# Moving two batches' transform stages by half a tile to a tile in a kernel that mixes a Fourier filter with routed experts

## Chip, core and metric

One core of one Trainium2 chip. The metric is the device time of one execution in microseconds, median of three runs. The program is built once; it computes everything in float32.

## What is computed

The reference filters a sequence in the frequency domain and sends each token through one of eight experts, chosen by a hash of its id:

```python
batch, seq, dim = (8, 2496, 256)
X = np.fft.rfft(x, axis=1)
F = (filt_r + 1j * filt_i)[None, :, :]
y = np.fft.irfft(X * F, n=x.shape[1], axis=1)
...
N, D, E, F = (19968, 256, 8, 1024)              # N = 8 * 2496 tokens
expert_idx = token_ids * np.int64(2654435761) % np.int64(E)
for e in range(E):
    mask = expert_idx == e
    h = np.maximum(y.reshape(N, D)[mask] @ w1[e], 0.0)
    out[mask] = h @ w2[e]
```

## The kernel before

The Fourier transform of 2496 = 39 x 64 points is done as matrix products with tables, in three stages per batch:

- stage 1 (`pa`): products of x with `wf`, evicted to a buffer in SBUF, which is then stored to a DRAM scratch `d1`;
- stage 2 (`pb`, filter, `pc`): `load2` brings `d1` back transposed (in the profile `mid<-d`), `forward` multiplies by `d_t` and VectorE applies the filter, `back` multiplies by `e_t`; the result is stored to a second scratch `d2`;
- stage 3 (`pd`): `load4` brings `d2` back transposed (`t<-d`), products with `wi_t`, and each row of tokens is scattered to its expert's place in the DRAM array `xs`.

```python
def stage1(self, u):
    ...
    self.products(wf_t, (NR, NR), 2 * NS, self.x[v][:, sl, :], self.t1[:, sl, :], nc.scalar.copy, u, "pa")
    if half == 1:
        eng = nc.scalar if self.b == 2 else nc.gpsimd
        moves = self.parts(self.d1, self.t1, v)
        if self.b == 2 and v > 0:
            put_off.extend(moves)            # batch 2: these stores are issued later, by ScalarE
            return
        for dram, chip in moves:
            eng.dma_start(out=dram, in_=chip)

def load2(self, g):
    t2 = slot("t2")
    for p in range(2):
        a0 = p * NS + SG * g
        nc.sync.dma_start(out=t2[p:P:2, :, :], in_=self.d1[:, a0:a0 + SG, :])
    self.t2[g] = t2

def load4(self, v):
    self.t4[v] = t4pool.tile([NK, XL, C], F32, name=f"t4_{self.b}_{v}", tag="t4")
    for dram, chip in self.parts(self.d2, self.t4[v], v):
        nc.sync.dma_start(out=chip, in_=dram)
```

Batches are numbered from 0: "the third batch" is batch 2, "the fourth" batch 3. The first two batches are transformed ahead of the main loop, on chip alone. The main loop then goes through tiles of 128 routed tokens, 159 of them without a condition. Each tile is an up product (`ups`, 32 matmuls), a down product (`dps`, 16) and a scatter of its rows to the output. The other six batches are transformed between the products of the tiles. The tiles come in four routing stages, and those of a routing stage need the tokens of two more batches: 30 tiles can run with batches 0 and 1, the next ones need batches 2 and 3 as well.

```python
def step(i):
    ht = work.tile([P, FP, TB], F32, name=f"ht_{i}", tag="ht")
    if i + 4 < NT:
        load(i + 4)                          # xg<-xs: the tokens of a tile (of a pair of tiles), on the sync queue
    numbers(i)
    while main and main[0][0] < i + .5:      # pieces of the transforms, by their times
        main.pop(0)[1]()
    up(i, ht)
    weights(i + 2, 0)                        # wts<-in_moe_w: loaded only if the expert changes
    if i + 1 < NSURE:
        turn(i + 1)                          # xt<-xg, VectorE
    while main and main[0][0] < i + 1:
        main.pop(0)[1]()
    down(i, ht)
    weights(i + 2, 1)
```

What is put between the products of which tile is set by hand: each piece has a time in units of tiles. A piece with time 8.55 is issued in tile 8 between up and down, one with 8.0 in tile 8 ahead of up. Negative times lie ahead of the loop. All loads are issued by the sync engine in the order of these times, and a load that must wait holds those behind it.

```python
def spaced(t0, t1, n):
    return [t0 + (t1 - t0) * u / n for u in range(n)]

def part1(b, at, loads=None):                # stage 1: times of its pieces, and of the loads of x
    bt = batches[b]
    if loads is None:
        loads = [at[2 * v] - 2.5 * (at[1] - at[0]) for v in range(NV)]
    return ([(at[u], lambda u=u: bt.stage1(u)) for u in range(NU)] +
            [(loads[v], lambda v=v: bt.load1(v)) for v in range(NV) if b > 0])

def part2(b, at, ready):                     # stage 2, and its loads: none ahead of "ready"
    bt = batches[b]
    if isinstance(ready, list):
        return ([(at[u], lambda u=u: bt.stage2(u)) for u in range(NS // 2 + 1)] +
                [(t, lambda g=g: bt.load2(g)) for g, t in enumerate(ready)])
    return ([(at[u], lambda u=u: bt.stage2(u)) for u in range(NS // 2 + 1)] +
            [(max(at[2 * g] - 4.5 * (at[1] - at[0]), ready), lambda g=g: bt.load2(g)) for g in range(NS // SG)])

def part3(b, at, ready=None):                # stage 3, and its loads: none ahead of "ready"
    ...
    return ([(at[u], lambda u=u: bt.stage3(u)) for u in range(NU)] +
            [(max(at[2 * v] - 2.5 * (at[1] - at[0]), ready), lambda v=v: bt.load4(v)) for v in range(NV)])
...
todo += [(-75.5, lambda: [nc.scalar.dma_start(out=dram, in_=chip) for dram, chip in put_off])]
todo += [(-76, lambda: begin())]             # the loads of the first four tiles
...
todo += [..., (14.6, pads)]                  # seven scatters of blank rows by GpSimd
```

Here `NU` = 6, `N_2` = 11, `NV` = 3. A piece of stage 2 with number u does `forward(u)` and then `back(u - 1)`.

Of the kernel before, what the change touches and what calls it, by code (L numbers as in the profile page):

```python
# [36 lines left out]
NU = (HN + XG) // XG  # L37
# [82 lines left out]
def kernel(  # L120
# [324 lines left out]
    def load_tables(part):  # L445
        if part < 2:

            nc.gpsimd.tensor_copy(junk[:], first.x[2 * part][0:1, 0, 0:1])
        sl = S_PARTS[part]
        nc.sync.dma_start(out=d_t[:, sl, :], in_=d_dram.ap()[:, sl, :])  # L450
        for k in range(2):
            load_filter(k, sl)
# [207 lines left out]
    def spaced(t0, t1, n):  # L660
        return [t0 + (t1 - t0) * u / n for u in range(n)]

    def part1(b, at, loads=None):
# [7 lines that stand above are left out]
    def part2(b, at, ready):  # L671
# [8 lines that stand above are left out]
    def part3(b, at, ready=None):  # L680
        bt = batches[b]
        if b < 2:
            return [(at[u], lambda u=u: bt.stage3(u)) for u in range(NU)]
        return ([(at[u], lambda u=u: bt.stage3(u)) for u in range(NU)] +
                [(max(at[2 * v] - 2.5 * (at[1] - at[0]), ready), lambda v=v: bt.load4(v)) for v in range(NV)])
# [4 lines left out]
    N_2 = NS // 2 + 1  # L690
# [8 lines left out]
    todo = [(t, lambda k=k: load_tables(k)) for k, t in enumerate((-160, -159, -157, -156))]  # L699
# [17 lines left out]
    todo += [(t, lambda k=k: weights(k // 2, k % 2)) for k, t in enumerate((-99, -98.9, -98.8, -98.7))]  # L717
    todo += [(-76, lambda: begin())]

    todo += part1(3, spaced(1.5, 6.5, NU), [-74.6, -74.5, 2.5]) + part1(4, spaced(15, 20.5, NU))  # L720
    todo += part1(5, spaced(21, 27, NU)) + part1(6, spaced(35, 44.5, NU)) + part1(7, spaced(50, 60, NU))
    todo += part2(2, spaced(.55, 6, N_2), [-75, -74.9, -74.8, -74.7, 1.2]) + part2(3, spaced(9.2, 15.7, N_2), 6.6)
    todo += part2(4, spaced(22, 31, N_2), 20.5) + part2(5, spaced(31.2, 46, N_2), 28)
    todo += part2(6, spaced(48, 62, N_2), 47) + part2(7, spaced(63.2, 80, N_2), 61)
    todo += part3(2, spaced(8, 14.5, NU), 5.8) + part3(3, spaced(17, 25, NU), 15.6)
    todo += part3(4, spaced(33, 44, NU), 31.5) + part3(5, spaced(49, 63, NU), 46.5)
    todo += part3(6, spaced(67, 83, NU), 62) + part3(7, spaced(84, 101, NU), 81)
    todo.sort(key=lambda t: t[0])
# [164 lines left out]
```

## Time and profile before

| | before |
|---|---|
| median of 3 runs | 1509.66 us (1508.82 to 1509.69) |
| span of the profiled run | 1507.1 us |
| granted TensorE clock, mean | 0.986 |
| the tile loop begins | 145.36 us |
| DMA engines, mean | 226.06 MB, 150 GB/s |

The profile names engines PE (TensorE matmul), PEld (TensorE weight load), DVE (VectorE), ACT (ScalarE), POOL (GpSimd) and SP (sync); SPq, ACTq and POOLq are what these engines' queues issue. `L799` is a line of the kernel. "out<-in" names what an instruction writes and reads, and x32 is the number of instructions of a group. Times are microseconds from the start of the span. In a list of waits, a line says who waited for whom, then the total, how often and the longest. In a timeline a line is start, length, engine, line, operation, count, and in brackets how long the engine was idle before it and what ended that. One line of matrix product in the kernel appears as two matmul records for each product of float32, so four `pb` are the two products of one piece.

Two places in the kernel before which the change touches: the pieces of batch 2's stage 2 begin in tile 0 (the first has time 0.55), with their loads and then the loads of x for batch 3 ahead of the loop; and the pieces of batch 3's stage 3 begin at tile 17, with their first load in tile 15.

### The profile page before, as it was taken

The page shows a single profiled execution, that of the slowest core. Times are in us where ns is not written, and L with a number is a line of the kernel's source. Part 1 is how long each engine was busy: PE and PEld are TensorE (multiplying, and loading weights), DVE is VectorE, ACT ScalarE, POOL GpSimd, SP SyncE. Part 2 cuts the span into 40 slices and gives each one's busy share as a digit, 9 for nine tenths or more (in the row PEclk, how much of TensorE's full clock was granted, in tenths as well). Part 3 has the DMA queues.
Part 4 walks back from the last instruction along what each step waited for, and adds up shares of the span by engine and source line. Part 5 has one row for each costly group of instructions (what it writes and reads, how often), then busy time and mean ns, then how long its engine had stood idle before and what let it go on. Part 6 is the DMA issues. An engine that isn't in the chain of part 4 may idle for free.

```text
span 1507.1 us, 25818 instructions
## 1 busy us (share of the span) xinstructions
PE 1454.8 (97%) x9340; PEld 1338.0 (89%) x9340; DVE 538.4 (36%) x1008; ACT 234.6 (16%) x401; POOL 495.2 (33%) x802
## 2 busy tenths in 40 slices
PE   6996899989999999999999999999999999999997
PEld 6885789988899998899899999899999999999996
DVE  5972444622444444143434442222222222212221
ACT  3653120111121111011111110000000000000000
POOL 6465123544422344233422433234212111111211
PEclk9998999999999999999999999999999999999998
DMA  8266758668855954846647623653422423132321
GB/s 225 56 203 179 250 181 216 231 174 247 245 178 181 270 149 116 241 134 195 178 124 204 194 96 117 164 157 91 138 57 61 131 88 90 48 109 71 98 86 28
DMA packets 186988, 226.06 MB, mean 150 GB/s; under 512 B 101653, under 2 KB 157389, under 8 KB 180890
## 3 DMA queue, kind: packets, MB, share of 16 engines
q1 hardware_dynamic: 154615, 146.92, 35.1%
q0 software_dynamic: 28096, 73.51, 15.1%
q10 hardware_dynamic: 4147, 3.94, 0.9%
q8 instruction: 76, 1.25, 0.3%
q14 instruction: 54, 0.44, 0.1%
HBM read 415.94 MB, written 75.08 MB: 326 GB/s over the span
## 4 chain that ended last, share of the span: by engine, by line
PE 90%; DMA 5%; DVE 2%; issue 1%; POOL 1%; SPq 0%; ACT 0%; ACTq 0%; POOLq 0%; DVEq 0%
PE ups L799 36%; PE dps L811 35%; PE pd L228 5%; PE pb L273 4%; PE pc L295 3%; PE pa L228 3%; DMA wts<-in_x_dram 1%; PE pc L345 1%; DMA wts<-in_moe_w_dram 1%; DMA t<-d 1%; DMA d_t<-d_tbl 1%; DMA d<-mid 1%; DMA mid<-d 1%; PE pu L360 1%; DVE z L282 1%
## 5 line engine op out<-in xcount | busy, mean ns | idle before, releaser
L799 PEld LDWEIGHTS ups<-xt,wts 128*128 128x128 f32 x5088 | 596.4, 193 | 22.4 <-POOL no L782 10.6
L799 PE MATMUL ups<-xt,wts 128*128 128x128 f32 x5088 | 597.8, 276 | 11.6 <-DVE xt L789 10.1
L811 PE MATMUL dps<-wts,ht 128*128 128x256 f32 x2544 | 577.0, 380 | 0.1
L811 PEld LDWEIGHTS dps<-wts,ht 128*128 128x128 f32 x2544 | 475.8, 191 | 62.0 <-ACT mid L298 0.8
L815 POOL DMA_INDIRECT out_dram<-osb,no x159 | 158.2, 995 | 555.3 <-DVE osb L814 461.1
L805 DVE TENSOR_SCALAR ht<-ups 128x512 f32<-128x512 f32 x159 | 110.0, 692 | 484.6 <-PE ups L799 478.4
L803 ACT ACTIVATE ht<-ups 128x512 f32<-128x512 f32 x159 | 94.9, 597 | 867.4 <-PE ups L799 852.9
L391 POOL DMA_INDIRECT xs<-o,sidx x176 | 176.6, 1003 | 98.2 <-issue 44.3
L814 DVE COPY osb<-dps 128x256 f32<-128x256 f32 x159 | 67.5, 425 | 365.5 <-PE dps L811 364.1
L782 POOL COPY no<-xg 32x2 int32<-32x2 int32 (+1 forms) x328 | 59.9, 183 | 269.0 <-DMA out_dram<-osb,no 183.2
L282 DVE TENSOR_TENSOR z<-pb,filt 64x512 f32<-64x512 f32 x160 | 110.1, 688 | 2.3
L228 PE MATMUL pd<-t,wi_t 120*117 120x256 f32 x320 | 77.9, 387 | 5.4 <-DMA t<-d 4.1
L789 DVE STREAM_TRANSPOSE xt<-xg 128x256 f32<-128x256 f32 x159 | 69.0, 434 | 14.7 <-DMA d<-mid 14.7
L228 PEld LDWEIGHTS pd<-t,wi_t 120*117 120x117 f32 x320 | 57.4, 183 | 18.2 <-issue 5.5
L298 ACT COPY mid<-pc 128x512 f32<-128x512 f32 x60 | 35.2, 586 | 233.3 <-PE pc L295 232.2
L279 DVE TENSOR_TENSOR y<-pb,filt 128x512 f32<-128x512 f32 x80 | 54.2, 678 | 47.7 <-PE pb L273 47.2
L273 PE MATMUL pb<-mid,d_t 128*128 128x256 f32 x240 | 63.8, 389 | 7.0 <-DMA mid<-d 7.0
L283 DVE TENSOR_TENSOR y<-y,z 128x512 f32<-128x512 f32 x80 | 61.2, 766 | 2.7
L295 PE MATMUL pc<-y,e_t 128*128 128x256 f32 x240 | 61.7, 379 | 0.0
L273 PEld LDWEIGHTS pb<-mid,d_t 128*128 128x128 f32 x240 | 44.3, 195 | 13.0 <-issue 5.4
L228 PE MATMUL pa<-x,wf_t 117*120 117x256 f32 x224 | 52.7, 379 | 0.0
L295 PEld LDWEIGHTS pc<-y,e_t 128*128 128x128 f32 x240 | 45.4, 190 | 6.5 <-issue 0.4
(123 smaller groups left out, 548.9 us busy)
## 6 DMA issues: line engine op xcount, KB each, us to landing
wts<-in_moe_w_dram SPq DMA_DIRECT2D x320, 1024.0 KB
mid<-d SPq DMA_DIRECT2D x60, 256.0 KB
d<-mid POOLq DMA_DIRECT2D x60, 256.0 KB, 3.9
xg<-xs SPq DMA_DIRECT2D x235, 64.0 KB
t<-d SPq DMA_DIRECT2D x12, 960.0 KB
x<-in_x_dram SPq DMA_DIRECT2D x36, 312.0 KB
d<-mid POOLq DMA_DIRECT2D x10, 960.0 KB, 8.8
xg<-xs SPq DMA_DIRECT2D x77, 65.0 KB
```

The lines of the kernel that those rows point to most:

```text
L228: nc.tensor.matmul(out=ps[0:cols * H, k, :], lhsT=w[:], rhs=src[:, 2 * i + k, :], start=True, stop=True)
L273: nc.tensor.matmul(out=ps[:, i, :], lhsT=d_t[:, s, :], rhs=rhs, start=True, stop=True)
L282: nc.vector.tensor_tensor(out=z[b], in0=ps[a], in1=f_t[1][a, sl, :], op=OP.mult)
L295: nc.tensor.matmul(out=ps[:, i, :], lhsT=e_t[:, 2 * u + i, :], rhs=pr[:, i, :], start=True, stop=True)
L391: st = nc.gpsimd.indirect_dma_start(out=xs[:], out_offset=bass.IndirectOffsetOnAxis(ap=index, axis=0), in_=rows, in_offset=None, bounds_ch ...
L789: nc.vector.transpose(out=xt[i].rearrange("p d (a t) -> p a d t", t=32), in_=xg[i][0][:, 4 * xg[i][1]:4 * xg[i][1] + 4, 0:C // 4].rearrang ...
L799: nc.tensor.matmul(out=ps[:, k, :], lhsT=w1[:, dp, fp * P:(fp + 1) * P], rhs=xt[i][:, dp, :], start=(dp == 0), stop=(dp == DP - 1))
L803: nc.scalar.activation(out=dst, in_=ps[:], func=AF.Relu)
L805: nc.vector.tensor_scalar_max(dst, ps[:], 0.0)
L811: nc.tensor.matmul(out=ps[:, 0, :], lhsT=ht[:, fp, :], rhs=w2[:, fp, :], start=(fp == 0), stop=(fp == FP - 1))
L814: nc.vector.tensor_copy(out=o[:], in_=ps[:, 0, :])
L815: st = nc.gpsimd.indirect_dma_start(out=out[:], out_offset=bass.IndirectOffsetOnAxis(ap=to_rows[i], axis=0), in_=o[:], in_offset=None, bou ...
```

## The change

Only times of pieces change, and so the order of instructions on each engine. Batch 2's stage 2 begins about a tile later (1.6 instead of 0.55), its stage 3 half a tile later, batch 3's stages 1, 2 and 3 by up to a tile, and the x of batch 3 (two of its three loads) is asked for ahead of the load for batch 2's stage 2 instead of behind it. The first loads for batch 6's stage 2 come 0.7 tiles earlier. It is meant to give the loads of stage 2 and stage 3 more time between their issue and their use.

```diff
-    todo += part1(3, spaced(1.5, 6.5, NU), [-74.6, -74.5, 2.5]) + part1(4, spaced(15, 20.5, NU))
+    todo += part1(3, spaced(2, 6.8, NU), [-75.3, -75.2, 3]) + part1(4, spaced(15, 20.5, NU))
     todo += part1(5, spaced(21, 27, NU)) + part1(6, spaced(35, 44.5, NU)) + part1(7, spaced(50, 60, NU))
-    todo += part2(2, spaced(.55, 6, N_2), [-75, -74.9, -74.8, -74.7, 1.2]) + part2(3, spaced(9.2, 15.7, N_2), 6.6)
+    todo += part2(2, spaced(1.6, 6.6, N_2), [-75, -74.9, -74.8, -74.7, 2.3]) + part2(3, spaced(9.4, 15.5, N_2), 6.6)
     todo += part2(4, spaced(22, 31, N_2), 20.5) + part2(5, spaced(31.2, 46, N_2), 28)
-    todo += part2(6, spaced(48, 62, N_2), 47) + part2(7, spaced(63.2, 80, N_2), 61)
-    todo += part3(2, spaced(8, 14.5, NU), 5.8) + part3(3, spaced(17, 25, NU), 15.6)
+    todo += part2(6, spaced(48, 62, N_2), 46.3) + part2(7, spaced(63.2, 80, N_2), 61)
+    todo += part3(2, spaced(8.55, 14.5, NU), 6.6) + part3(3, spaced(17.6, 25.1, NU), 16.2)
     todo += part3(4, spaced(33, 44, NU), 31.5) + part3(5, spaced(49, 63, NU), 46.5)
     todo += part3(6, spaced(67, 83, NU), 62) + part3(7, spaced(84, 101, NU), 81)
```

## The prediction

> **What bounds the kernel now.** First the page: shares of busy time, then the chain that ended last.
>
> ```profile
> PE 1454.8 (97%) x9340; PEld 1338.0 (89%) x9340; DVE 538.4 (36%) x1008; ACT 234.6 (16%) x401; POOL 495.2 (33%) x802
> PE 90%; DMA 5%; DVE 2%; issue 1%; POOL 1%; SPq 0%; ACT 0%; ACTq 0%; POOLq 0%; DVEq 0%
> ```
>
> TensorE (PE) is the bound: 97% of the span, and 90% of the chain. The change adds no matmul and removes none, so only the other 3% (1507.1 - 1454.8 = 52 us) and what the clock loses behind a pause can be won. The next view is what the PE waited for over the whole run (total us, times, longest):
>
> ```profile
> PE ups L799 <- DVE xt L789: 10.1, 1, 10.1
> PE pb L273 <- DMA mid<-d: 7.0, 2, 4.8
> PE pd L228 <- DMA t<-d: 4.1, 1, 4.1
> ```
>
> The first is the start of the tile loop, which the change leaves alone. The other two are three pauses, all for a transposing load: two for stage 2 (pb), one for stage 3 (pd). The timeline of the PE shows where they lie (start us, length, idle before it in brackets):
>
> ```profile
> 145.36 6.46 PE L799 MATMUL ups<-xt,wts 128*128 128x128 f32 x32 [10.11 <-DVE xt L789]
> 156.62 2.04 PE L273 MATMUL pb<-mid,d_t 128*128 128x256 f32 x4 [4.80 <-DMA mid<-d]
> 158.46 4.95 PE L811 MATMUL dps<-wts,ht 128*128 128x256 f32 x16
> 163.25 1.03 PE L273 MATMUL pb<-mid,d_t 128*128 128x256 f32 x4
> ...
> 330.75 3.62 PE L811 MATMUL dps<-wts,ht 128*128 128x256 f32 x16
> 338.47 3.57 PE L228 MATMUL pd<-t,wi_t 120*117 120x256 f32 x8 [4.10 <-DMA t<-d]
> 341.83 3.85 PE L799 MATMUL ups<-xt,wts 128*128 128x128 f32 x32
> 345.52 1.89 PE L228 MATMUL pa<-x,wf_t 117*120 117x256 f32 x8
> ```
>
> The third pause (2.22 us, in a stretch that I read separately) lies before the pb at 639.06. A pause costs more than its idle time: what follows is slow. From start to start, four pb, sixteen dps, eight pd or pa and 32 ups take 0.86, 3.45, 1.73 and 3.57 us elsewhere in this timeline. So:
> - First pause: from the end of the ups at 151.82 to the pb at 163.25 are 11.43 us, for work of 0.86 + 3.45: 7.1 lost.
> - Second: 4.10 idle, pd 3.36 instead of 1.73, ups 3.69 instead of 3.57: 5.9 lost.
> - Third: 2.2 idle, pb 1.87 instead of 0.86, ups 4.30 instead of 3.57: 4.0 lost.
>
> Together 17.0 us, 1.1% of the time. That is the ceiling for all that the change aims at.
>
> The fourth view is the timeline of the queues: what ScalarE, the sync engine (SP) and GpSimd (POOL) issued around the first and second pause, which shows why the loads were late:
>
> ```profile
> 144.06 2.93 ACTq L716 DMA_DIRECT2D d<-mid  x3
> 152.81 4.97 SPq L264 DMA_DIRECT2D mid<-d  x8
> 157.88 4.96 SPq L210 DMA_DIRECT2D x<-in_x_dram  x6
> ...
> 323.45 1.14 POOL L302 DMA_DIRECT2D d<-mid  x2
> 326.80 0.38 SPq L372 DMA_DIRECT2D t<-d  x1
> 327.70 5.62 SPq L765 DMA_DIRECT2D xg<-xs  x4
> ```
>
> The stage-2 load of the third batch goes out at 152.81 because the put-off stores of its stage 1, begun at 144.06, land only at 152.66 (the chain has "145.52 7.14 DMA d<-mid" there); its first pair lands at 156.49, 3.8 us later. The stage-3 load of the fourth batch goes out at 326.80, when the last store of its stage 2 (323.45) has landed, and takes 11.5 us.
>
> **What the Trainium skill says.** TensorE: Matmul & The Clock Gate, section Part 1: The HAM clock gate: an idle PE falls to half clock after about 3.4 us and needs about as long of work to get it back. The trace agrees with the half (granted clock 0.50 from 156 to 160 us), but the fall comes sooner: 0.58 on average from 154 to 156, hence at about 154.3, 2.5 us after the PE stopped; at the third pause, 0.75 from 638 to 640, after about 2.3. DMA: Bandwidth & Descriptors, section Anatomy of one DMA: the issuing sequencer holds a semaphore wait before dispatch, so a blocked load also holds everything behind it in program order. The trace agrees: the x loads at 157.88 follow the blocked mid load at once, though their buffers were free. The same page, Queues, rings and completion order: a DMA engine takes turns between queues packet by packet. Nothing in this trace tests what that does between the ScalarE and the sync queue.
>
> **The change part by part.** It moves instructions only; I compared the order of both programs on each engine.
>
> *First pause.* The first pb moves from behind ups 0 to behind ups 1, so it is wanted at 145.36 + 6.46 (ups 0, cold) + 3.45 (dps 0) + 3.57 (ups 1) = 158.8, 7.0 us later than the 151.8 of before. With the loads as they were (156.49) the pause would be gone. But the six x loads now go out ahead of the mid load, at about 143.8, because the first pa is wanted 4.3 us after the pb and could not have had them otherwise. They carry 6 x 312 KB = 1.87 MB and run beside the 1.6 MB of stores (960 + 600 + 40 KB), while the DMA engines are already 0.93 to 0.97 busy (144 to 150 us). At the 262 GB/s that the 154 to 170 us windows average for the mid and x loads, x takes 7.1 us of them. If it came wholly first, the stores would land at 152.7 + 7.1 = 159.8; if the added queue filled gaps, at perhaps 155. I choose 157.6 (5 us late, an estimate). The first pair of mid then lands at 157.6 + 3.8 = 161.4, and pb waits 2.6, about long enough to lose the clock: 1.0 for half of the 2.3 lost to it before. Left 3.6 of 7.1: gain 3.5.
>
> *Second pause.* The first pd of the fourth batch moves behind ups 17, the last pc from behind ups-dps 14 to between them. On the axis of before, dps 15 ends at 325.45; then ups 16 (3.57), pa (1.73), dps 16 (3.45), ups 17 (3.57): pd is wanted at 337.8 instead of 334.2. On GpSimd the seven blank scatters start about 1 us earlier, and the last store no longer stands behind a result scatter: it should go out at about 321.4 and land 2.6 us later, at 324. The load however now stands behind four xg loads of its tile, which can go only after dps 15 and take about 1.9 us (a set of four at 371.51 took 1.87): issue at 327.5. With the 11.5 us of before it lands at 339.0, 1.2 late; with less of the 960 KB store of the next batch beside it, perhaps 9.5, in time. I take 0.7 left of 5.9: gain 5.2.
>
> *Third pause.* Four of the six loads of the seventh batch's stage 2 move from the tile where they are needed to the tile before, ahead of a 960 KB t load. They follow the xg loads that end at 626.3, and land by about 626.3 + 3.8 = 630 to 632, where pb wants them at 636.8. Windows show the DMA engines at 0.66 and 0.21 just there. Gain 4.0. The t load goes out some 2.4 us later (four issues of 0.6); its pd comes at 648.7, so that is hidden.
>
> *Third batch's stage 3.* Its last pc moves back by 68.9 - 64.7 = 4.2 us of PE work, its first pd by 3.6. Load to use shrinks by half a microsecond or less from some 13; no wait was there, I expect none.
>
> Sum: 3.5 + 5.2 + 4.0 = 12.7; 1509.66 - 12.7 = 1497.0.
>
> **The rivals.**
> - *x in front just moves the pause.* If x comes wholly before the stores, pb gets its data at 163.6, waits 4.8 and pays the clock again: nothing is won at the first place, total about 1500.5. For it: the engines are near full, and x packets are of 8 KB against 1 KB of the stores. Against it: only 2.0 MB moved from 143 to 153 us (203 GB/s), while 338 GB/s are reached at 160 to 162.
> - *All three pauses vanish.* Then 17.0 are won, 1492.7. For it: the stretch at 152 to 154 us has the DMA engines at 0.02, so x ahead fills time that was empty.
> - *The weights of tile 3 become the wait.* That load (1 MB, issued at 176.96 for ups at 191.12) now stands behind both xg sets and the mid loads. I put its issue at about 172 and its use at about 184; if it slips by more than 5 us there is a new wait of a few us, total about 1500.
> - *The t load stays late* because it now follows xg: with 11.5 us and later stores there remain 2 us and a cold clock, total about 1500.
>
> **Range and chances.** 1497 with 8 in 10 between 1490.5 and 1504. The low end is the full 17.0 with 2 us of luck in other waits; the high end is the first pause kept, the second two thirds kept. Over 2% faster would need 30 us, more than the three pauses hold; over 2% slower a new wait of 30 us, which nothing suggests.
>
> **What would show it.** In the profile after: the pb wait near 158 to 162 (mine: 2.6 us; gone if x did not disturb; 4.8 if it did fully), the landing of the put-off stores (157.6), the pd wait near 335 (0.7), no pb wait near 620 to 640. PE busy time should fall by what the cold stretches cost, idle by the rest. I am wrong if a new pause appears in tiles 2 to 12, above all on weights or on t of the third batch, or if the loads of the second routing stage, which follow the last scatter of the fourth batch, come later.

## The result, and the profile after

| | before | changed |
|---|---|---|
| median of 4 runs | 1509.24 us (1507.56 to 1509.69) | 1500.65 us (1499.08 to 1501.95) |
| span of the profiled run | 1507.1 us | 1497.7 us |
| tile loop begins | 145.36 us | 145.14 us |
| from there to the end | 1361.7 us | 1352.6 us |

The ratio is 0.9945, 95% interval 0.9927 to 0.9962: 0.4 to 0.7% faster. The prediction was 1497.0, in a range of 1490.5 to 1504.

The start of the tile loop is not at the same time in every run (144.2 to 148.0 us in e1 to e8 and e12, 153.1 to 159.7 in e9 to e11). For a question of a few microseconds I therefore compare the time from the first `ups` of tile 0 to the end, below called the loop time.

The page of the changed kernel, shares of busy time and the chain that ended last:

```profile
PE 1451.6 (97%) x9340; PEld 1336.5 (89%) x9340; DVE 536.9 (36%) x1008; ACT 234.7 (16%) x401; POOL 501.2 (33%) x802
PE 92%; DMA 5%; DVE 1%; issue 1%; SPq 0%; POOL 0%; ACTq 0%; ACT 0%; DVEq 0%; POOLq 0%
```

PE is busy 3.2 us less: stretches that ran on the slow clock are gone. The rest of the 9.4 us of span was idle time. What the PE waited for over the run:

```profile
PE ups L799 <- DVE xt L789: 10.1, 1, 10.1
PE pb L273 <- DMA mid<-d: 5.4, 1, 5.4
...
PE pd L228 <- DMA t<-d: 0.6, 1, 0.6
```

Of three pauses one is still there, one is nearly gone and one is gone. The PE timeline, first where the first pause was, then the second, then the third (the pb at 631.61 is the one that waited before):

```profile
145.14 6.62 PE L799 MATMUL ups<-xt,wts 128*128 128x128 f32 x32 [10.06 <-DVE xt L789]
151.60 3.62 PE L811 MATMUL dps<-wts,ht 128*128 128x256 f32 x16
155.06 3.73 PE L799 MATMUL ups<-xt,wts 128*128 128x128 f32 x32
164.15 2.05 PE L273 MATMUL pb<-mid,d_t 128*128 128x256 f32 x4 [5.36 <-DMA mid<-d]
165.99 4.67 PE L811 MATMUL dps<-wts,ht 128*128 128x256 f32 x16
170.50 1.89 PE L228 MATMUL pa<-x,wf_t 117*120 117x256 f32 x8
...
334.42 3.73 PE L799 MATMUL ups<-xt,wts 128*128 128x128 f32 x32
338.75 1.98 PE L228 MATMUL pd<-t,wi_t 120*117 120x256 f32 x8 [0.60 <-DMA t<-d]
...
631.61 1.03 PE L273 MATMUL pb<-mid,d_t 128*128 128x256 f32 x4
```

The pb is now two products later, and waits all the same. From the end of ups 1 (158.79) to the pa at 170.50 are 11.71 us for work of 0.86 + 3.45: 7.4 lost, against 7.1 before. The queues tell why:

```profile
143.16 9.61 SPq L210 DMA_DIRECT2D x<-in_x_dram  x6
144.97 4.57 ACTq L716 DMA_DIRECT2D d<-mid  x3
160.11 4.98 SPq L264 DMA_DIRECT2D mid<-d  x8
...
326.04 4.50 SPq L765 DMA_DIRECT2D xg<-xs  x4
330.79 0.36 SPq L372 DMA_DIRECT2D t<-d  x1
```

The mid load goes out at 160.11, when the put-off stores land (the chain has "146.15 13.88 DMA d<-mid" there). From the loop's start that is 15.0 us, against 7.4 before (152.81 - 145.36). So the x loads in front made the stores 7.5 us later, just what moving pb had won.

### The profile page after: what moved, and what is told of

Same layout as the page of the kernel before. It is cut to its first block, busy times and chain, and to the rows that moved or that the text cites. A ratio compares the mean times of both kernels' runs of the same rounds, so it can differ in the third digit from the quotient of the medians.

```text
span 1497.7 us, 25814 instructions
## 1 busy us (share of the span) xinstructions
PE 1451.6 (97%) x9340; PEld 1336.5 (89%) x9340; DVE 536.9 (36%) x1008; ACT 234.7 (16%) x401; POOL 501.2 (33%) x802
## 4 chain that ended last, share of the span: by engine, by line
PE 92%; DMA 5%; DVE 1%; issue 1%; SPq 0%; POOL 0%; ACTq 0%; ACT 0%; DVEq 0%; POOLq 0%
PE ups L799 37%; PE dps L811 36%; PE pd L228 5%; PE pb L273 4%; PE pc L295 3%; PE pa L228 3%; DMA wts<-in_x_dram 1%; PE pc L345 1%; DMA d<-mid 1%; DMA wts<-in_moe_w_dram 1%; DMA d_t<-d_tbl 1%; PE pu L360 1%; PE pa L324 1%; PE pd L222 1%; DMA t<-d 1%
## 5 line engine op out<-in xcount | busy, mean ns | idle before, releaser
L228 PEld LDWEIGHTS pd<-t,wi_t 120*117 120x117 f32 x320 | 56.4, 181 | 13.2 <-ACT o L230 1.3
```

The lines of the kernel that those rows point to most:

```text
L228: nc.tensor.matmul(out=ps[0:cols * H, k, :], lhsT=w[:], rhs=src[:, 2 * i + k, :], start=True, stop=True)
```

## The experiments

Every loop time below is the span less the start of the first `ups` of tile 0, both of the same profile. Each comes from one profile, so differences of a microsecond are not to be read from it (by its medians e4 gains 2.8 us, by its loop time 3.8). "mid out" is the issue of the first mid load, from the loop's start.

| run | mid out | first PE wait for data in tiles 0 to 2 | loop time |
|---|---|---|---|
| before | 7.4 | pb 4.8 | 1361.7 |
| changed | 15.0 | pb 5.4 | 1352.6 |
| e1, both x behind | 7.4 | pa 4.6 | 1352.4 |
| e2, one x ahead | 10.0 | pb 0.6 | 1346.3 |
| e3, x behind one mid pair | 7.2 | weights 1.4 | 1347.6 |
| e4, third pause alone | 7.5 | pb 4.7 | 1357.9 |
| e12, e2 and pd later | 10.2 | pb 0.5 | 1345.9 |

**e1, the x loads back behind the mid load.**

```diff
-    todo += part1(3, spaced(2, 6.8, NU), [-75.3, -75.2, 3]) + ...
+    todo += part1(3, spaced(2, 6.8, NU), [-74.6, -74.5, 3]) + ...
```

> The changed kernel with the two x loads of the fourth batch behind the four pairs of mid loads again, as before the change. Theory (the x loads ahead take the DMA engines from the put-off stores): the stores land near 152.5 instead of 160.0, the first mid pair near 156.5, and the first pb, wanted at 158.8, does not wait. The first pa, wanted at about 163.2, then waits for its x, issued from 157.9 on and landing between 163.5 and 166: 0 to 3 us. Total 4 to 7 us below the changed kernel, about 1494 to 1497. Rival (the stores are late for another cause, such as the order on the ScalarE queue or the mid load being slow in itself): stores still near 160, the pb wait stays near 5, total about 1501 or above.

Measured: 1501.42 us, ratio 0.9949 (0.9929 to 0.9969). The mid load goes out as early as in the kernel before, and pb does not wait: the x loads did hold up the stores. But pa waits 4.6 us for its x, more than the 0 to 3 expected, and starts on a cold clock; so the total of 1494 to 1497 that I expected was missed. The timeline of the PE in e1:

```profile
160.11 1.03 PE L273 MATMUL pb<-mid,d_t 128*128 128x256 f32 x4
160.98 3.62 PE L811 MATMUL dps<-wts,ht 128*128 128x256 f32 x16
169.23 3.39 PE L228 MATMUL pa<-x,wf_t 117*120 117x256 f32 x8 [4.64 <-DMA x<-in_x_dram]
```

So x both ahead and both behind cost the same 1352.5: the pause only changes its name.

**e2, one of the two x loads ahead.**

```diff
+    todo += part1(3, spaced(2, 6.8, NU), [-75.3, -74.5, 3]) + ...
```

> The changed kernel with one of the two x loads (936 KB of 1.87 MB) ahead of the mid load and the other behind it. Theory: the delay of the stores goes with the bytes in front: they land half as late, at about 156.5 instead of 152.5 (none ahead) or 160.0 (both ahead); first mid pair at 160.3, pb waits about 1.5 us and keeps most of its clock, total about 5 us below the changed kernel. Rival (any x ahead spoils it, because the packets of x are large and win every turn until the x queue is empty and the stores have a tail of their own): landing at 158 or later, wait above 3 us, total within 3 us of the changed kernel.

Measured: 1494.80 us, ratio 0.9908 (0.9890 to 0.9925). With half the bytes ahead the mid load is 2.6 us late instead of 7.5, so less than half; pb waits 0.57, the clock stays up, and pa has its x. Timeline of the PE in e2:

```profile
158.12 1.10 PE L273 MATMUL pb<-mid,d_t 128*128 128x256 f32 x4 [0.57 <-DMA mid<-d]
...
162.51 1.89 PE L228 MATMUL pa<-x,wf_t 117*120 117x256 f32 x8
```

This version is faster than both kernels: 6.3 us of loop time below the changed one.

**e3, the first x load between the mid pairs.**

```diff
+    todo += part1(3, spaced(2, 6.8, NU), [-74.95, -74.5, 3]) + ...
```

> The changed kernel with the first x load behind the first pair of mid loads and the second behind all four pairs. Theory: stores land near 152.5, first mid pair near 156.5, no wait of pb at 158.8; x for pa goes out at about 154 and lands by 161, before it is wanted at 163.2; so the whole first pause (7.4 us with its cold clock) is gone: total about 1493.5. Rival (the pause is only handed on): a wait of 3 us or more appears at the second pair of pb, near 170, or at tile 3's weights, total above 1497.

Measured: 1497.48 us, ratio 0.9925 (0.9907 to 0.9943). Neither pb nor pa waits, as the theory had it, but the rival holds in part: the ups of tile 2 wait 1.41 us "for the weights":

```profile
170.66 3.84 PE L799 MATMUL ups<-xt,wts 128*128 128x128 f32 x32 [1.41 <-DMA wts<-in_moe_w_dram]
170.52 0.12 SPq L422 DMA_DIRECT2D wts<-in_moe_w_dram  x1
```

That load is not carried out at all (its issue takes 0.12 us, where one that is carried out takes 0.38), but the sync engine comes to it only at 170.52, behind mid, x and xg, and the ups can start at 170.66.

**e4, the third pause alone.**

```diff
-    todo += part2(6, spaced(48, 62, N_2), 47) + ...      (the kernel before)
+    todo += part2(6, spaced(48, 62, N_2), 46.3) + ...
```

> The kernel before with only the first loads for the seventh batch's stage 2 moved from 47 to 46.3. Theory: the third pause of 2.2 us and the cold clock behind it go, 4.0 us in all, and the two other pauses stay: about 1505.3. Rival (the lead of the load is eaten elsewhere): under 2 us.

Measured: 1506.21 us, ratio 0.9981 (0.9973 to 0.9989). The loop time falls by 3.8 us, close to the theory's 4.0; the medians differ by only 2.8. The pauses at pb (4.7) and pd (4.0) stay.

**e5, only the later pd** (from the kernel before).

```diff
-    ... part3(3, spaced(17, 25, NU), 15.6)
+    ... part3(3, spaced(17.6, 25.1, NU), 15.6)
```

> The kernel before with only the pieces of the fourth batch's stage 3 moved half a tile later (17.6 to 25.1), their load still ready at 15.6 and so ahead of the xg loads. Theory (the later use alone removes the second pause): the t load lands as before, 11.5 us after it goes out, some 4 us after the end of dps 16; pd is wanted 3.6 us later, so the wait is 0.3 to 0.8 us and the clock stays up. Rival (the earlier store of the last stage-2 piece is what counts): the wait stays near 3 to 4.

Measured in one run: pd waits 0.36 us, so the later use alone takes the wait away. But a new one comes 24 us later:

```profile
341.32 1.99 PE L228 MATMUL pd<-t,wi_t 120*117 120x256 f32 x8 [0.36 <-DMA t<-d]
365.65 5.30 PE L811 MATMUL dps<-wts,ht 128*128 128x256 f32 x16 [2.12 <-DMA wts<-in_moe_w_dram]
```

The wait and the cold clock behind it (5.30 instead of 3.62) cost 3.8 us. In this run the second t load, 960 KB, goes out at 344.28, just ahead of the two weight loads that dps needs (348.83 and 349.53). In the kernel before it goes out at 333.37, which is 8.6 us earlier from the loop's start. That this is the cause was not tried.

**e6, only the earlier store** (from the kernel before). Of this stage the first pieces move later and the last ones earlier.

```diff
-    ... part2(3, spaced(9.2, 15.7, N_2), 6.6)
+    ... part2(3, spaced(9.4, 15.5, N_2), 6.6)
```

> The kernel before with only the pieces of the fourth batch's stage 2 moved to 9.4 to 15.5, so that the last store of that stage goes out ahead of a result scatter of GpSimd; stage 3 and its load as before. Theory (the store is worth less than the later use): store out about 2 us earlier, t load out about 2 to 2.6 us earlier, pd waits 1.5 to 2 instead of 4.1. Rival: the wait is gone, or unchanged because the t load is limited by the DMA engines.

Measured in one run: the t load goes out 2.4 us earlier, but pd still waits 3.31; the wait got 0.8 shorter, not the 2.1 to 2.6 expected. From the loop's start, t goes out at 181.4 in the kernel before, at 179.1 here, and at 185.7 in the changed kernel, behind the xg loads. By the chain it has landed at 193.0, 192.1 and 193.6. Issue differs by 6.6 us, landing by 1.4, so its turn in the sync queue is not what sets the landing. In the kernel before, from 326 to 330 us, the DMA engines were taken by GpSimd's queue (q0), with the 960 KB store of the next batch that GpSimd had issued at 324.58; the sync queue (q1), where t went out at 326.80, hardly moved (packets, MB, share of 16 engines):

```profile
q0 software_dynamic: 231, 0.81, 87.9%
q1 hardware_dynamic: 12, 0.01, 1.4%
```

That store goes out at nearly the same place in the loop in all three kernels (179.2, 178.3 and 178.8 us from its start), so it may be what sets the landing of t. Moving it was not tried.

**e7 and e8, pieces of 512 bytes and of 4 KB.** Each x load of the changed kernel split in two, by channels or by rows:

```diff
+ for k in range(2):                                        # e7: pieces of 512 bytes
+     nc.sync.dma_start(out=xt[h:NR:H, 0:n, k * P:(k + 1) * P], in_=...[[N2 * C, N1], [C, n], [1, P]])
+ for k in range(2):                                        # e8: pieces of 4 KB
+     nc.sync.dma_start(out=xt[h:NR:H, 4 * k:4 * k + 4, :], in_=...[[N2 * C, N1], [C, 4], [1, C]])
```

> The changed kernel with each of its six x loads split in two by halves of the 256 channels, so that the pieces in a row are of 512 bytes instead of 8 KB; bytes, order and buffers are the same. Theory (the engines take turns between the queues piece by piece, and pieces of 8 KB beat the stores' pieces of 1 KB): with small pieces the stores win, and land 11 us or less after the tile loop's start (14.9 in the changed kernel, 7.3 in the kernel before). Rival (the bytes count, whatever the pieces): 14 us or later.

> The control to the run with 512-byte pieces: each x load split in two by rows, so that there are as many issues, with pieces of 4 KB. Theory: as in the changed kernel, 13 to 15 us after the tile loop's start. Rival (the number of issues and their rate set the delay, not the pieces): the same landing as with 512 bytes, whatever that is.

Measured in one run each: the mid load goes out 13.6 (e7) and 13.3 us (e8) from the loop's start, when the sync engine has issued the last x (15.2 and 15.3 us for twelve issues). It did not wait for the stores then, so their landing is only bounded. The ScalarE queue's share in the DMA engines shows when they ended (packets, MB, share of 16 engines). In e8 from 156 to 158 us, 11.3 to 13.3 from the loop's start:

```profile
q10 hardware_dynamic: 1, 0.00, 0.0%
```

In e7 from 158 to 160, 11.2 to 13.2 from the loop's start:

```profile
q10 hardware_dynamic: 10, 0.01, 1.5%
```

With 4 KB the stores end no later than with 512 bytes. My theory that the size of the pieces decides has fallen. The rival in e8, that the number of issues and their rate set the delay, fits: the changed kernel issued the same bytes in 9.6 us. The loop times are 1350.2 us (e7, where pb waits 0.67 but dps 0 waits 2.0 ahead of it) and 1352.1 (e8, where pb waits 4.5). The same view from 146 to 148 us, in the kernel before (the stores alone) and then in the changed one (q1 is the sync queue):

```profile
q10 hardware_dynamic: 447, 0.46, 93.3%
```

```profile
q1 hardware_dynamic: 73, 0.43, 69.4%
q10 hardware_dynamic: 112, 0.11, 21.5%
```

In these two microseconds the stores moved 0.46 MB before and 0.11 MB after. In e8, where each issue carries half the bytes, x moved 0.11 MB in that window and the stores 0.41.

The landing goes with how much x had moved by then, counted from the loop's start: no x in the kernel before (7.4 us), 0.89 MB in e2 (10.0), 1.2 to 1.4 MB in e8 and e7 (11 to 13), 1.89 MB in the changed kernel (15.0). That is an order and no proof, and bytes are not all: in the changed kernel the stores had only 7.2% of the engines from 156 to 158 us and 3.8% from 158 to 160, while all queues together held 0.44 and 0.26 of them. What kept the last stores is not shown.

**e9 and e10, the first and the second pause alone**, from the kernel before: e9 has stages 1 of the fourth and 2 and 3 of the third batch at their new times, with one x load ahead; e10 has the fourth batch's stages 2 and 3 as in the changed kernel.

```diff
+ e9:  part1(3, spaced(2, 6.8, NU), [-75.3, -74.5, 3]); part2(2, spaced(1.6, 6.6, N_2), [..., 2.3]); part3(2, spaced(8.55, 14.5, NU), 6.6)
+ e10: part2(3, spaced(9.4, 15.5, N_2), 6.6); part3(3, spaced(17.6, 25.1, NU), 16.2)
```

> The kernel before with only the first pause's part of the change (stages 1 of the fourth and 2 and 3 of the third batch later), and one x load of two ahead of the mid loads. Theory (the three pauses are independent): pb waits under 1 us after ups 1, pa does not wait, the waits of 4.1 at pd near 335 and 2.2 at pb near 635 stay; the time from the start of the tile loop to the end falls from 1361.7 by 6 to 7 us. Rival (the second and third batch's stages later bring a new wait): under 4 us, with a wait above 2 us in tiles 6 to 12.

> The kernel before with the fourth batch's stages 2 and 3 and their loads moved as in the changed kernel, nothing else. Theory (t behind the xg set keeps the weights' place in the queue): pd waits 0.5 to 1.2 us, no wait for weights near 365, and the time from the tile loop's start falls from 1361.7 by 4.5 to 5.5 us. Rival (the later pd alone brings the wait for weights that the run of the later pd showed, 2.1 us and a cold clock): under 3 us.

Measured in one run each, on a chip where the kernel before took 1515 to 1525 us; so only waits are read. In e9 pb waits 0.20, pa not at all, and the third pause stays with 2.6; pd waits 0.84 and not 4.1; a dps ahead of it had itself stood still for 1.8 us, which may be why. In e10 pb waits 5.2 and pd 1.5, more than expected, and no wait for weights follows near pd: with t behind the xg loads the pause was not handed on as in e5, in this one run. The gains of 6 to 7 and of 4.5 to 5.5 us stay unmeasured.

**e11 and e12, the best version.** e2, and the first pd 0.2 tiles later:

```diff
+    third = part3(3, spaced(17.6, 25.1, NU), 16.2)
+    todo += [(17.8, third[0][1])] + third[1:]
```

> The changed kernel with one of the two x loads ahead of the mid load, and the first pd of the fourth batch 0.2 tiles later, behind a pa. Theory (the t load lands at a time that the DMA traffic sets, some 193.5 us after the tile loop's start): pd is wanted 1.7 us later and no longer waits the 1.0 of the run with one x load ahead; total 0.5 to 1.2 us below that run, 1493.6 to 1494.3, and a ratio near 0.990. Rival (pd is held by its place behind the xg loads, or the wait is handed on): no gain, or a new wait at the weights near 360.

> The same kernel as in the run before, whose comparison was scattered (the kernel before took 1515 to 1525 us there). Theory: no wait of PE for the t load near 330 and at most 0.6 us at the first pb; the time from the tile loop's start to the end is 1345 to 1346, a microsecond below the 1346.3 of the run with one x load ahead; ratio to the kernel before 0.989 to 0.991. Rival (the gain at pd is handed on): a new wait, and 1346.3 or above.

Measured: e11, on the chip of e9 and e10, 1507.97 us, ratio 0.9914 (0.9888 to 0.9939); e12, 1492.19 us, ratio 0.9910 (0.9893 to 0.9926). The waits of the PE in the loop of e12, behind its start:

```profile
PE ups L801 <- DMA wts<-in_moe_w_dram: 1.5, 1, 1.5
PE pd L228 <- ACT mid L230: 0.7, 1, 0.7
PE pb L273 <- DMA mid<-d: 0.5, 1, 0.5
```

The wait for t is gone, and 0.7 us of another has come: pd now follows a pa at once and waits for ScalarE to evict it. 0.4 us of loop time remain, below what the runs resolve; e2 and e12 can't be told apart.

## Why the prediction was right in sum, point by point

| step | predicted gain | measured |
|---|---|---|
| first pause | 3.5 of 7.1 | -0.3 |
| second pause | 5.2 of 5.9 | 5.2 |
| third pause | 4.0 of 4.0 | 4.0 (alone: 3.8) |
| start of the loop | 0 | 0.2 |
| sum | 12.7 | 9.1 (span: 9.4; medians: 8.6) |

- *What bounds it* was right: PE is the bound, and what was won is idle time of PE and cold clock behind it. The ceiling of 17.0 was nearly reached by e2 (15.4) and e12 (15.8).
- *First pause*: the mechanism was the predicted one, the mis-sized term is the delay of the stores. I put 5 us between 2 and 7; it was 7.5, so nothing was won where I had 3.5. The rival "x in front just moves the pause" was right in what came of it. But x did not come wholly first, as that rival had it: the stores got 21.5% of the engines from 146 to 148 us, where they had had 93.3%, and then 64 to 79% until 154, with x beside them at 17 to 30%. Two parts of the delay were in no estimate. ScalarE came to the stores 0.2 us ahead of the loop's start instead of 1.3, as its four xg loads took 3.19 us to issue and not 2.33; and the last stores moved slowly from 156 to 160 us although the engines were less than half busy. That 7.5 lies near the rival's 7.1, which is bytes over rate, is therefore in part luck. e2 shows that the delay is not simply in proportion: half the bytes cost a third.
- *Second pause*: the 0.7 us left are right (0.60 idle, and 0.09 on the pd), but by two errors that cancel. The t load went out at 330.8 and not 327.5, because the set of four xg took 4.5 us and not 1.9; and it took 7.9 us and not 9.5 to 11.5. In e6 too its landing hardly depended on its issue.
- The share of the earlier store was small (0.8 us of wait in e6), that of the later use large (3.7 in e5). The place behind xg goes with no wait for weights (e10), where the later pd alone had one (e5).
- *Third pause*: right.
- *The sum* lies in the range because its high end allowed for a first pause that stays; nothing else made up for it.
- *Third batch's stage 3* and *weights of tile 3*: no wait came there. The weight load went out at 174.5 (predicted about 172), 13.4 us ahead of its ups at 187.9.
- *The Trainium skill*, TensorE: Matmul & The Clock Gate, Part 1: The HAM clock gate, has the PE fall to half clock after about 3.4 us of idleness. The changed kernel shows about 2.5: granted 1.00 from 158 to 160 and 0.82 from 160 to 162, idle from 158.8. But the 2.5 and 2.3 of the prediction are no rule. In e5 the clock fell 2.0 us after the PE stopped (idle from 363.5, granted 0.75 from 365 to 366), in e1 only after about 5.0 (idle from 164.6, granted 1.00 until 169 and 0.80 from 169 to 170), and another wait in e5, 2.33 us ahead of the pb at 640.44, left it at 1.00. Waits of under 1.5 us (e2, e3, pd of the changed kernel) cost no clock. DMA: Bandwidth & Descriptors, Queues, rings and completion order, says that an engine takes turns packet by packet; that the size of pieces would therefore decide was my inference, and e7 and e8 speak against it.

## What to carry to other kernels

Here a load that was asked for earlier took the DMA engines from the store that the next load waited for, and the pause just moved. Look for what runs beside an earlier load, and ask ahead only for what is needed first: half of x ahead won 6.3 us over all of it and 6.1 over none of it. Where the landing of a load hardly moved with its issue, as that of t, an earlier issue was worth 0.8 us of wait and a later use 3.7; but the later use brought a new wait for weights in e5, so read the loads that follow as well.

## What was not expected of the hardware

- The time to issue the same stores differed with the other traffic, and ScalarE came to its next work only behind it. The three put-off stores took ScalarE 2.93 us to issue before, 4.57 with x ahead, and 8.28 in e7, where ScalarE then came so late to evict tile 0 that dps waited 2.0 us (what held the issue is not shown):

```profile
146.35 8.28 ACTq L721 DMA_DIRECT2D d<-mid  x3
154.68 0.60 ACT L808 ACTIVATE ht<-ups 128x512 f32<-128x512 f32 x1 [17.38 <-DMA d<-mid]
```

- In e3 a weight load that was skipped by its condition gave its go-ahead only when the sync engine reached it (1.41 us of PE).
- The same t load took 11.5, 13.1 and 7.9 us (before, e6, changed) for 960 KB, and landed within 1.4 us of the same place in the loop.
